# Key sums with v as the stationary side, two heads side by side, and token sums added on GpSimd

## The chip, the cores and the metric

The kernel runs on one core of one Trainium2 chip. The metric is the device time of one execution in microseconds, as the median of several runs; lower is better. The inputs are fp32 and come from a fixed seed.

## The reference

Random-feature attention over 8 batches of 8 heads with 576 tokens and head size 64, followed by a softplus MLP. The features are exp of a projection on 128 directions, less half the squared norm, less the row's maximum. Per head, the keys' features give a matrix `kv` (128 x 64) and a vector `z` (128), the sum of the features over the tokens.

```python
proj = np.einsum('bhsd,md->bhsm', x, omega)
h = proj - np.sum(x * x, axis=-1, keepdims=True) / 2.0
phi = np.exp(h - np.max(h, axis=-1, keepdims=True)) / np.sqrt(m)
kv = np.einsum('bhsm,bhsd->bhmd', k_p, v)
z = np.sum(k_p, axis=2)
num = np.einsum('bhsm,bhmd->bhsd', q_p, kv)
den = np.einsum('bhsm,bhm->bhs', q_p, z)[..., None] + 1e-06
x = (num / den).transpose(0, 2, 1, 3).reshape(B * S, H * D)   # 4608 x 512
g = softplus(x @ w_in)                                        # 512 -> 2048
out = g @ w_out                                               # 2048 -> 512
```

## The kernel before

**Work and tiles.** The MLP takes its 4608 tokens in blocks: two of 256, then eight of 512. For each block and each of 16 chunks of the hidden layer, TensorE computes layer 1 (`plan_step`, L1412 to L1414), ScalarE and VectorE compute the softplus, and TensorE adds the chunk to layer 2 (L1441 to L1443). Each operand is split in a high and a low part of a reduced fp32 format, so three products stand for one. The last two blocks are done as a pair with seven products in place of eight (`plan_pair`).

The attention is done in quads: four heads of one batch, 16 quads in all. A quad's tokens come in five units: units 0 to 3 hold 128 tokens of each of the four heads, unit 4 holds the last 64 tokens, with two heads on top of each other on the 128 partitions. The quads of the first batch have a path of their own (`plan_early_keys`, `plan_early_queries`); the change leaves it alone but for priorities. In the 14 later quads a unit is loaded, squared for its norms, projected (`plan_unit` for the second batch, `plan_split` with L588 from the third on), and its features are made by ScalarE (L495, L612).

**The sums over the keys** (`plan_sums`). For each later quad there are two bursts on TensorE, at L676: one over units 0 to 2, one over units 3 and 4. In a product the features of one head (128 tokens x 128 features) are the stationary side and v with a column of ones (65 columns) streams; unit 4 streams 130 columns for two heads, which are kept apart by zeros in v. The operands are full fp32, and the profile shows two instructions for each product. The result has features on the partitions and, for each head, 64 columns of `kv` and one column of `z`. ScalarE takes the first burst's result out of PSUM (`part`, L682). VectorE adds the second: `z` (L686) and `kv` (`whole`, L694). The four columns of `z` are turned by a 32 x 32 transpose (L690), go to DRAM in four transfers (L700), and come back spread over all partitions (L704). A query unit multiplies its features with that and sums (`den`, L784), takes the reciprocal (L790), divides (L794, on GpSimd or VectorE), turns blocks of 32 (L798), and goes through DRAM (L808, L821) to the products with `kv` (L954, L997, L1048): there 64 columns of `kv` are stationary, and the two heads of a pair write the upper and the lower 64 partitions of one bank.

**What sets the order.** Nothing is scheduled by hand. Each piece of work is put on a list with `do(engine, cost, due, emit, after=..., take=..., give=...)`; `in_order` runs through the list with a simple model of the engines (costs, lags, free buffers) and issues, on each engine, among the works that can start the one with the earliest `due`. The `due` numbers and the tables at the top (`KEYS`, `QUERIES`, `IN`, `OUT`) are the priorities. `take` and `give` name buffers; a buffer is free again when the work that gives it is done. The order that comes out is fixed at build time, and each engine executes it in order. GpSimd and VectorE share a port: each GpSimd work waits for the last VectorE work marked `port` that was issued ahead of it.

Of the kernel before, what the change touches and what calls it, by code (L numbers as in the profile page):

```python
# [50 lines left out]
KEYS = ((-130.35, -33.11, -44.26, -126.91, -51.00), (-184.12, -170.41, -56.38, -80.88, -261.61))  # L51
QUERIES = ((-121.36, -68.53, -68.01, 5.46, 8.94), (-154.85, -144.78, -170.95, 8.02, 66.23))
IN = (-77.35, -86.63, -115.20, 17.77, 69.89, -10.45, 6.40, 31.06, 149.98, 21.85, 124.48, 208.49, 408.59, 38.21, 62.49, 277.15)
OUT = (-17.17, 0.51, -6.07, 4.04, -17.23, 9.28, 112.67, 220.08, 30.78, 8.68, 46.33, 97.42, 71.82, 129.46, 148.54, 186.47)
# [47 lines left out]
def in_order(works, room, ahead, margin):  # L102
# [11 lines left out]
    first, out = 0, []  # L114
    port, queue, flying = [0.0, "POOL"], [0.0], [0.0] * MOST
# [28 lines left out]
    while len(out) < len(works):  # L144
# [26 lines left out]
        for box, key in w.give:  # L171
            free[box[key]] = w.done, e
            held[box[key]][-1][1::2] = w.done + lag(e, "PE"), len(out)
# [36 lines left out]
def favor_softplus_kernel(ctx, tc, q0, k0, qx, qy, kx, ky, vv, om, wi, wo, out):  # L210
# [57 lines left out]
    z_wide = [at.tile([P, 32], F32, name=f"z{i}") for i in range(2)]  # L268
    for t in z_wide:
        nc.vector.memset(t, 0.0)  # L270

    stack = const.tile([P, D], F32, name="stack")
# [42 lines left out]
    def plan_weights(nm, fc, due):  # L315
# [36 lines left out]
        def low_part(e):  # L352
# [5 lines left out]
            "SP", dma(0.65, 1.60, 1.7), due + 87.17, load, spare={} if last else {"w": 2},  # L358
# [5 lines left out]
        a = do(("ACT", "DVE"), (aw + 0.03, dw2), due + 3.12, low_bits, after=[l], port=True)  # L364
        b = do("ACT", aw + 0.03, due + 18.05, rebias, after=[l])
        c = do("DVE", dw, due + 9.50, joined, after=[a, b], port=True)
        d = do(
            ("ACT", "DVE"), (aw, dw2), due + 19.59, high_part, after=[c] + (in_w if last else []), take=[("w", box, "w")], port=True,
# [3 lines left out]
        return do(("DVE", "POOL"), (dw, pw), due - 0.32, low_part, after=[d], give=[(box, "raw")], port=True)  # L372
# [13 lines left out]
    def plan_unit(q, kind, us, due, early):  # L386
# [32 lines left out]
        def load_v(i):  # L419
            b["v", i] = wide(at.tile([P, 272], F32, name=f"v{nm}_{i}", tag=b["vs", i], bufs=1))  # L420
            nc.sync.dma_start(b["v", i], vv[q.b - 1, q.qd][:, 4 * us[i] : 4 * us[i] + 4])
# [8 lines left out]
        def norms():  # L430

            sm = b["sm"] = at.tile([P, 4, 8], F32, name=f"sm{nm}", tag=b["sms"], bufs=1)
# [230 lines left out]
    def plan_sums(q, keys, due, deps):  # L663
# [4 lines left out]
        def outer(k):  # L668
            b, i, u = keys[k]
            if not k:  # L670
                y["kv"] = wide(bank(f"kv{q.nm}_{q.sums}_{first}", y["bank"]))
# [1010 lines left out]
```

## Time and profile before

| | before |
|---|---|
| median of 3 runs | 996.43 us (996.05 to 996.76) |
| span of the profiled execution, first to last instruction | 995.2 us |
| median of the runs less that span | 1.2 us |
| TensorE busy | 989.6 us, 99% |
| weight loads of TensorE busy | 830.9 us, 83% |
| VectorE busy | 783.6 us, 79% |
| ScalarE busy | 722.7 us, 73% |
| GpSimd busy | 206.4 us, 21% |
| granted clock of TensorE, mean | 1.000 of full speed |

The busy times are sums over one execution that the profiler recorded. The profile gives no separate device time for that execution, so its span is set beside the median of the runs. Weight loads run beside products and have a row of their own. In the rows below PE is TensorE, PEld its weight loads, DVE VectorE, ACT ScalarE, POOL GpSimd and SP the engine that issues the transfers. In a timeline a row that ends in x16 is a run of 16 instructions of one line; matmuls overlap, so the start of the next row, and not the duration, says how long a run held the engine.

### The profile page before, as it was taken

The numbers are of one execution on the slowest core, as the hardware profiler recorded it, in microseconds if no ns is written. First come the engines' busy times: TensorE is split into PE (matmuls) and PEld (weight loads), VectorE is DVE, ScalarE is ACT, GpSimd is POOL, SyncE is SP. The second block draws the span as 40 slices with busy tenths as digits, with TensorE's granted clock in tenths as the row PEclk, the third lists the DMA queues.
The fourth block names the chain that finished last, engine by engine and source line by source line (L and its number), as shares of the span: only waits on it lengthen the run. The fifth ranks groups of instructions, "written<-read, shape, count | busy, mean of one in ns | idle before, by whom it ended". The sixth has DMA issues, their size and how long they took to land.

```text
span 995.2 us, 17488 instructions
## 1 busy us (share of the span) xinstructions
PE 989.6 (99%) x5495; PEld 830.9 (83%) x5495; DVE 783.6 (79%) x2306; ACT 722.7 (73%) x1794; POOL 206.4 (21%) x235
## 2 busy tenths in 40 slices
PE   9999999999999999999999999999999999999998
PEld 8988888888888888888878888888888878888886
DVE  6899986889898888888879886887787958676620
ACT  7999887879777777877777776776776656666520
POOL 3313232312221122101212121112011214223000
PEclk9999999999999999999999999999999999999999
DMA  9982355454464455543454444434542331000011
GB/s 321 352 282 90 111 162 152 138 160 141 136 183 139 125 138 160 159 128 113 138 144 133 123 129 119 155 106 113 138 141 75 80 92 43 0 1 1 1 43 42
DMA packets 117628, 124.49 MB, mean 125 GB/s; under 512 B 16288, under 2 KB 93728, under 8 KB 117536
## 3 DMA queue, kind: packets, MB, share of 16 engines
q1 hardware_dynamic: 117392, 123.26, 41.4%
q8 instruction: 43, 0.70, 0.3%
q14 instruction: 49, 0.40, 0.1%
q10 hardware_dynamic: 144, 0.13, 0.0%
HBM read 97.37 MB, written 25.98 MB: 124 GB/s over the span
## 4 chain that ended last, share of the span: by engine, by line
PE 98%; DVE 1%; ACT 0%; issue 0%
PE banks L1441 11%; PE banks L1412 11%; PE banks L1442 10%; PE banks L1443 10%; PE banks L1413 10%; PE banks L1414 10%; PE banks L1199 8%; PE banks L676 5%; PE banks L588 5%; PE banks L1256 3%; PE banks L1258 3%; PE banks L1257 3%; PE banks L445 2%; PE banks L997 2%; PE banks L735 1%; PE banks L954 1%
## 5 line engine op out<-in xcount | busy, mean ns | idle before, releaser
L1412 PE MATMUL banks<-xh,wi 128*128 128x512 f32 (+1 forms) x512 | 188.8, 369 | 0.4 <-DVE u L1427 0.4
L1413 PE MATMUL banks<-xl,wi 128*128 128x512 f32 (+1 forms) x512 | 186.1, 363 | 0.0
L1414 PE MATMUL banks<-xh,wi 128*128 128x512 f32 (+1 forms) x512 | 185.9, 363 | 0.0
L1441 PE MATMUL banks<-wo,gh 128*128 128x512 f32 x448 | 178.6, 399 | 0.0
L1442 PE MATMUL banks<-wo,gh 128*128 128x512 f32 x448 | 175.5, 392 | 0.0
L1443 PE MATMUL banks<-wo,gl 128*128 128x512 f32 x448 | 175.0, 391 | 0.0
L1418 ACT ACTIVATE u<-banks 128x512 f32<-128x512 f32 (+1 forms) x128 | 70.1, 548 | 73.4 <-PE banks L1414 60.5
L1412 PEld LDWEIGHTS banks<-xh,wi 128*128 128x128 f32 x512 | 96.4, 188 | 17.2 <-issue 1.2
L1414 PEld LDWEIGHTS banks<-xh,wi 128*128 128x128 f32 x512 | 96.4, 188 | 15.6
L1413 PEld LDWEIGHTS banks<-xl,wi 128*128 128x128 f32 x512 | 96.6, 189 | 13.9
L1441 PEld LDWEIGHTS banks<-wo,gh 128*128 128x128 f32 x448 | 84.2, 188 | 18.5 <-issue 4.3
L1443 PEld LDWEIGHTS banks<-wo,gl 128*128 128x128 f32 x448 | 84.1, 188 | 18.5
L1442 PEld LDWEIGHTS banks<-wo,gh 128*128 128x128 f32 x448 | 84.4, 188 | 13.3
L1427 DVE SCALAR_TENSOR_TENSOR u<-banks,u 128x512 f32<-128x512 f32 (+1 forms) x128 | 78.4, 613 | 15.8 <-ACT u L1424 15.4
L612 ACT ACTIVATE phq<-phq,smq 128x128 f32<-128x128 f32 x216 | 71.8, 395 | 14.7 <-DVE smq L608 14.7
L794 POOL TENSOR_TENSOR phq<-phq,dnq 128x512 f32<-128x512 f32 (+1 forms) x46 | 41.9, 911 | 189.2 <-DVE dnq L790 113.1
L612 ACT ACTIVATE phk<-phk,smk 128x128 f32<-128x128 f32 x216 | 71.9, 397 | 10.7 <-DVE smk L608 10.7
L784 DVE CUSTOM_DVE_ANT_0 restq<-phq,zb 128x128 f32<-128x128 f32 x280 | 72.7, 293 | 4.8 <-ACT phq L612 4.0
L1421 ACT ACTIVATE u<-u 128x512 f32<-128x512 f32 (+1 forms) x128 | 74.4, 581 | 1.8
L1424 ACT ACTIVATE u<-u 128x512 f32<-128x512 f32 (+1 forms) x128 | 74.6, 584 | 1.3
L1431 ACT CAST gh<-u 128x512 fp32r<-128x512 f32 (+1 forms) x97 | 55.8, 576 | 18.0 <-PE banks L1442 17.1
L1435 POOL TENSOR_TENSOR gl<-u,gh 128x512 fp32r<-128x512 f32 (+1 forms) x41 | 45.1, 1101 | 106.4 <-ACT gh L1431 31.5
(224 smaller groups left out, 2097.3 us busy)
## 6 DMA issues: line engine op xcount, KB each, us to landing
xk<-ky SPq DMA_DIRECT2D x48, 384.0 KB
xq<-qy SPq DMA_DIRECT2D x48, 384.0 KB
qdq<-restq SPq DMA_DIRECT2D x56, 256.0 KB
out<-o SPq DMA_DIRECT2D x36, 256.0 KB
vk<-vv SPq DMA_DIRECT2D x70, 130.0 KB
rawi<-wi SPq DMA_DIRECT2D x16, 512.0 KB
rawo<-wo SPq DMA_DIRECT2D x16, 512.0 KB
q<-qdq SPq DMA_DIRECT2D x64, 128.0 KB
```

The source lines that it names most:

```text
L612: nc.scalar.activation(b["ph"][:, c], b["ph"][:, c], AF.Exp, bias=b["sm"][:, 2, c : c + 1])
L784: i = nc.vector.tensor_tensor_reduce(jk[r, c], ph[r, c], q.zb[r, h], 1.0, 1e-6, ALU.mult, ALU.add, dn[r, 0, c : c + 1])
L1199: nc.tensor.matmul(b[key], x, y, start=fresh and not kk and not n, stop=kk == 1 and n == 2, skip_group_check=True)
L1412: nc.tensor.matmul(b["h"], wh, xh[:, cc, t], start=cc == 0, stop=False)
L1413: nc.tensor.matmul(b["h"], wh, xl[:, cc, t], start=False, stop=False)
L1414: nc.tensor.matmul(b["h"], wl, xh[:, cc, t], start=False, stop=cc == NCC - 1)
L1421: nc.scalar.activation(b["u"], b["u"], AF.Exp, scale=-1.0)
L1424: nc.scalar.activation(b["u"], b["u"], AF.Ln, bias=1.0)
L1427: nc.vector.scalar_tensor_tensor(b["u"], b["h"], 0.0, b["u"], ALU.max, ALU.add)
L1441: nc.tensor.matmul(acc[tt], gh, w2[fc][:, 0], start=fc == 0, stop=False)
L1442: nc.tensor.matmul(acc[tt], gh, w2[fc][:, 1], start=False, stop=False)
L1443: nc.tensor.matmul(acc[tt], gl, w2[fc][:, 0], start=False, stop=fc == NFC - 1)
```

## The change

For the 14 later quads the two sides of the key sums change places. v (64 columns of one head) is stationary and the features (128 columns) stream; the two heads of a pair write the lower and the upper 64 partitions of the same columns. Unit 4 has two products with 128 stationary columns, v of two heads side by side with zeros for the rows of the other head. The result has the columns of v on the partitions, so it is turned back by two TensorE transposes (`kv_turn`) after `part` and `whole`, and copied from PSUM to `kvs` by ScalarE or VectorE (`kv_turned`).

`z` is no longer a column of the products. GpSimd adds the features of the units into a tile for each quad (`plan_z`: unit 0 and 1, then 2, 3, and the two halves of unit 4). In `kv_turn` four products with a 128 x 32 block of ones add that up over the tokens, one head for each 32 partitions; ScalarE or VectorE copies the result (`z_row`), one transfer takes it to DRAM, and it is read back as before. The factor 1/128 of `z` moves into `den`. The buffers of the features are now given back by two works, the product and the addition, which `in_order` counts (`shared`). v is loaded with 64 columns in place of 65. Feature pieces of 320 tokens are loaded as 256 and 64. `z` has one buffer in place of two. All priorities have new values, and the rounding of the split units is put in a fixed order (`prev["rounded"]`).

```diff
-KEYS = ((-130.35, -33.11, -44.26, -126.91, -51.00), (-184.12, -170.41, -56.38, -80.88, -261.61))
+KEYS = ((-360.00, -109.33, -152.22, -165.69, -143.98), (-411.64, -277.96, -235.62, -203.68, -278.02))
...
         for box, key in w.give:
-            free[box[key]] = w.done, e
+            left, last = shared.get((id(box), key), (box.get(("uses", key), 1), (0.0, e)))
+            left, last = shared[id(box), key] = left - 1, max(last, (w.done, e))
+            if left:
+                continue
+            free[box[key]] = last
...
+    def plan_z(q, b, i, u, due, es):
+        b["uses", ("phs", i)] = 2
+        if not u:
+            q.z_first, q.z_slots = (b, i, es), {}
+            return
+        def add():
+            add_ = nc.gpsimd.tensor_tensor
+            x = b["ph", i]
+            if u == 1:
+                q.z = at.tile([P, 4, M], F32, name=f"z{q.nm}", tag="z", bufs=1)
+                b0, i0, _ = q.z_first
+                return add_(q.z, b0["ph", i0], x, ALU.add)
+            if u < 4:
+                return add_(q.z, q.z, x, ALU.add)
+            for j in (1, 0):
+                r, h = slice(j * D, (j + 1) * D), slice(2 * j, 2 * j + 2)
+                a_ = add_(q.z[r, h], q.z[r, h], x[r, :2], ALU.add)
+            return a_
...
+        q.z_last = do(
+            "POOL", pool(512) if u < 4 else 2 * pool(256), due - 200.04, add, after=after, give=give,
+            take=[("z", q.z_slots, "z")] if u == 1 else [],
+        )
...
         def outer(k):
...
-            for c in range(4 if u < 4 else 2):
-                end = k == len(keys) - 1 and c == (3 if u < 4 else 1)
-                cs = slice(c, c + 1) if u < 4 else slice(c, 4, 2)
-                nc.tensor.matmul(kv[:, cs], ph[:, c], v[:, cs], start=not k and not c, stop=end, skip_group_check=True)
+            end = k == len(keys) - 1
+            if u == 4:
+                for p in range(2):
+                    nc.tensor.matmul(kv[:, p], v[:, 2 * p : 2 * p + 2], ph[:, p], start=False, stop=end, skip_group_check=True)
+                return
+            for p in range(2):
+                for j in range(2):
+                    c = 2 * j + p
+                    nc.tensor.matmul(
+                        kv[j * D : (j + 1) * D, p], v[:, c], ph[:, c], start=not k and not p, stop=end, skip_group_check=True
+                    )
...
-        def z():
-            q.z = z_wide[int(q.slots["z"][-1])][:, :4]
-            nc.vector.scalar_tensor_tensor(q.z, y["kv"][:, :, D], rm, q.kvp[:, :, D], ALU.mult, ALU.add)
-        def z_turn():
-            nc.vector.transpose(q.zr, z_wide[int(q.slots["z"][-1])])
         def whole():
+            nc.vector.scalar_tensor_tensor(q.kvp, y["kv"], rm, q.kvp, ALU.mult, ALU.add)
+        def kv_turn():
+            y["turned"] = y["bank"][:, 2 * M :].rearrange("p (a m) -> p a m", m=P)
+            for p in range(2):
+                nc.tensor.transpose(y["turned"][:, p], q.kvp[:, p], ident)
+            for c in range(4):
+                nc.tensor.matmul(
+                    y["bank"][32 * c : 32 * (c + 1), :M], ones.broadcast_to([P, 32]), q.z[:, c], start=True, stop=True,
+                    skip_group_check=True,
+                )
+        def kv_turned(e):
+            (nc.scalar.copy if e == "ACT" else nc.vector.tensor_copy)(
+                q.kvs, y["turned"].rearrange("p a (j d) -> p (a j) d", d=D)
+            )
+        def z_row(e):
+            (nc.scalar.copy if e == "ACT" else nc.vector.tensor_copy)(q.z[:, 0], y["bank"][:, :M])
         def out_z():
-            for i in range(4):
-                r = slice(i * 32, (i + 1) * 32)
-                nc.sync.dma_start(q.zd[:, r], q.zr[i * 32 : i * 32 + 4])
+            nc.sync.dma_start(q.zd, q.z[::32, 0])
...
-        a = do("DVE", 0.1, due - 204.75, z, after=[m, q.part], take=[("z", q.slots, "z")])
-        q.kvl = do("DVE", 0.35, due - 85.10, whole, after=[m, a] + old, give=[(y, "bank")])
-        a = do("DVE", 0.11, due + 295.40, z_turn, after=[a])
-        r = do("SP", dma(2.0, 0.4, 1.4, 4), due - 43.15, out_z, after=[a], give=[(q.slots, "z")])
+        a = do("DVE", 0.35, due - 330.34, whole, after=[m, q.part])
+        y["uses", "at"] = 2
+        a = do("PE", 0.55, due - 96.36, kv_turn, after=[a, q.z_last], heat=512)
+        q.turned_kv = a
+        q.kvl = do(("ACT", "DVE"), (act(2 * P, PSUM), dve(2 * P)), due + 194.57, kv_turned, after=[a] + old, give=[(y, "at")])
+        a = do(("ACT", "DVE"), (act(M, PSUM), dve(M)), due - 364.83, z_row, after=[a], give=[(y, "at")])
+        r = do("SP", dma(2.0, 0.4, 1.4), due - 275.50, out_z, after=[a], give=[(q.z_slots, "z")])
...
-                        jk[r, c], ph[r, c], q.zb[r, h], 1.0, 1e-6, ALU.mult, ALU.add, dn[r, 0, c : c + 1]
+                        jk[r, c], ph[r, c], q.zb[r, h], 1.0 / M, 1e-6, ALU.mult, ALU.add, dn[r, 0, c : c + 1]
...
-            sizes = [w] if w <= 320 else [256, w - 256]
-            kinds = ["q" if w <= 256 else "q1"] if w <= 320 else ["q0", "q1"]
+            sizes = [w] if w <= 256 else [256, w - 256]
+            kinds = ["q"] if w <= 256 else ["q0", "q1"]
```

## Rows read from the trace of the kernel before

**Rows 1.** The page, part 1: busy us (share of the span) and instructions of each engine.

```profile
PE 989.6 (99%) x5495; PEld 830.9 (83%) x5495; DVE 783.6 (79%) x2306; ACT 722.7 (73%) x1794; POOL 206.4 (21%) x235
```

**Rows 2.** The page, part 4: the chain that ended last, by engine.

```profile
PE 98%; DVE 1%; ACT 0%; issue 0%
```

**Rows 3.** Waits of TensorE: total us, times, longest us (behind the first layer-1 product).

```profile
PE banks L1412 <- DVE u L1427: 0.4, 1, 0.4
```

**Rows 4.** Busy us by stretch: sum, PE, PEld, DVE, ACT, POOL, PEclk, DMA share, GB/s.

```profile
200.00:300.00 100.00, 100.00 (x539) 84.01 (x538) 90.24 (x287) 78.78 (x206) 22.00 (x24) 1.00 0.54 156
```

**Rows 5.** Timeline of TensorE, last product: start us, duration us.

```profile
990.98 0.39 PE L1258 MATMUL banks<-wo,wi 128*128 128x512 f32 x1
```

**Rows 6.** Timeline of TensorE around the two key-sum bursts of a quad.

```profile
196.30 0.39 PE L1414 MATMUL banks<-xh,wi 128*128 128x512 f32 x1
196.53 2.79 PE L676 MATMUL banks<-vk,phk 128*128 128x65 f32 x24
199.12 0.48 PE L1441 MATMUL banks<-wo,gh 128*128 128x512 f32 x1
199.44 0.39 PE L1442 MATMUL banks<-wo,gh 128*128 128x512 f32 x1
199.67 0.39 PE L1443 MATMUL banks<-wo,gl 128*128 128x512 f32 x1
...
212.99 1.50 PE L676 MATMUL banks<-vk,phk 128*128 128x65 f32 x12
214.25 0.48 PE L1441 MATMUL banks<-wo,gh 128*128 128x512 f32 x1
214.56 0.40 PE L1442 MATMUL banks<-wo,gh 128*128 128x512 f32 x1
```

**Rows 7.** Timeline of TensorE around three half-width bursts of query products.

```profile
668.90 0.39 PE L1443 MATMUL banks<-wo,gl 128*128 128x512 f32 x1
669.22 1.09 PE L954 MATMUL banks<-q,kvs 128*64 128x128 f32 x16
670.24 0.50 PE L1441 MATMUL banks<-wo,gh 128*128 128x512 f32 x1
670.58 0.40 PE L1442 MATMUL banks<-wo,gh 128*128 128x512 f32 x1
...
384.17 1.95 PE L954 MATMUL banks<-q,kvs 128*64 128x256 f32 x16
386.05 0.50 PE L1441 MATMUL banks<-wo,gh 128*128 128x512 f32 x1
...
719.78 0.39 PE L1443 MATMUL banks<-wo,gl 128*128 128x512 f32 x1
720.10 1.78 PE L997 MATMUL banks<-q,kvs 128*64 128x256 f32 x16
721.81 0.50 PE L1412 MATMUL banks<-xh,wi 128*128 128x512 f32 x1
722.15 0.40 PE L1413 MATMUL banks<-xl,wi 128*128 128x512 f32 x1
```

**Rows 8.** Timeline of TensorE, first batch: full-width fp32 products and transposes.

```profile
23.62 2.06 PE L735 MATMUL banks<-xk 128*128 128x128 f32 x16
25.52 0.60 PE L868 MATMUL banks<-ident,xq 128*128 128x128 f32 x4
25.95 1.04 PE L735 MATMUL banks<-xk 128*128 128x256 f32 x4
```

**Rows 9.** Groups by form, GpSimd: count, busy us, mean ns, idle before it.

```profile
L1435 POOL TENSOR_TENSOR gl<-u,gh 128x512 fp32r<-128x512 f32 x27 | 34.9, 1291 | 66.4 <-ACT gh L1431 17.9 <-DVE gh L1431 10.7 <-PE banks L588 9.7
```

**Rows 10.** Timeline of all engines: a second burst, and VectorE's sum behind it.

```profile
360.02 1.50 PE L676 MATMUL banks<-vk,phk 128*128 128x65 f32 x12
...
362.51 0.42 DVE L694 SCALAR_TENSOR_TENSOR kvs<-banks,kvp 128x256 f32<-128x256 f32 x1
```

**Rows 11.** Waits of all engines: GpSimd's division for VectorE's reciprocal.

```profile
POOL phq L794 <- DVE dnq L790: 113.1, 25, 13.1
```

More of the change, by code (lines that the diff above doesn't have):

```diff
@@ L933, in plan_early_x @@
         t = do(
-            "PE", 0.45 if tail else 0.46, due - 227.12, turn, after=[d for _, d in rows], heat=1024, behind=prev.get("turn_x"),
+            "PE", 0.45 if tail else 0.46, due - 244.69, turn, after=[d for _, d in rows], heat=1024, behind=prev.get("turn_x"),
             take=[("any", y, "b")], give=[(b, "x") for b, _ in rows],
@@ L1349, in plan_pair @@
-            q2 = do(*dp(2 * P), sdue - 139.44, lambda e, b=b: sums(e, 2, b), after=[q1, f1], port=True)
-            q3 = do(*dp(2 * P), sdue - 44.26, lambda e, b=b: sums(e, 3, b), after=[q2], give=[(b, ("tag", "f2"))], port=True)
-            q4 = do(*dp(2 * P), sdue - 32.45, lambda e, b=b: sums(e, 4, b), after=[q2], port=True)
+            sdue = due - 87.40
+            f1 = do(*dp(TB), sdue - 125.62, lambda e, b=b, j=j, nm=nm: whole(e, b, "f1", j, nm), after=gate + [done_w["i", j]], take=[("two", b, ("tag", "f1"))], port=True, behind=pe.get((5, j - 2)))
@@ new lines, in plan_pair @@
+            f2 = do(*dp(TB), sdue - 164.91, lambda e, b=b, j=j, nm=nm: whole(e, b, "f2", j + H, nm), after=gate + [done_w["i", j + H]], take=[("two", b, ("tag", "f2"))], port=True, behind=f1)
+            q1 = do(*dp(2 * P), sdue + 217.42, lambda e, b=b, nm=nm: sum1(e, b, nm), after=[f2], take=[("two", b, ("tag", "R"))], port=True)
+            q2 = do(*dp(2 * P), sdue - 274.51, lambda e, b=b: sums(e, 2, b), after=[q1, f1], port=True)
+            q3 = do(*dp(2 * P), sdue - 178.03, lambda e, b=b: sums(e, 3, b), after=[q2], give=[(b, ("tag", "f2"))], port=True)
@@ L1357, in plan_pair @@
+            l34 = do(*dp(TB), sdue - 353.47, lambda e, b=b, j=j: low34(e, j, b), after=[h34], give=[(b, ("tag", "f1"))], port=True)
             last = j == H - 1
             tg = [(late["tag"], ("th", p, l)) for p in range(2) for l in range(2)] if last else []
[L1359 to L1361 removed]
@@ new lines, in plan_pair @@
+            p7 = prod(7, "C", True, due - 337.85, [l34] + late["done"][3], kind=hp, give=tg)
+            s7 = do(*cp, due + 126.52, lambda e, b=b, nm=nm: copied(e, b, "C", "s7", nm), after=[p7], take=[("two", b, ("tag", "s7"))])
+            p5 = prod(5, "A", False, due - 128.66, [s2] + late["done"][1], give=[(b, ("tag", "L"))])
+            c22 = do("DVE", dve(TB), due - 123.42, lambda b=b: added(b["s7"], b["A"], b["s7"]), after=[p5, s7])
+            p4 = prod(4, "C", False, due - 160.26, [s7] + late["done"][4])
@@ L1481, in store @@
                 nc.sync.dma_start(out[t0 + tt * P : t0 + (tt + 1) * P, :], o["t"])
-            a = do("DVE", 0.34, due - 79.90, left, after=[ends[tt]], take=[("ph" if last else "t2", o, "s")])
-            r = do("ACT", 0.27, due - 143.96, right, after=[ends[tt]] if last and tt == n // P - 1 else [a], give=[(box, ("acc", i, tt))])
-            do("SP", dma(0.25, 0.8, 1.05), due - 76.25, store, after=[a, r], give=[(o, "s")], late=LATE["store"])
+            a = do("DVE", 0.34, due - 449.59, left, after=[ends[tt]], take=[("ph" if last else "t2", o, "s")])
+            r = do("ACT", 0.27, due - 458.35, right, after=[ends[tt]] if last and tt == n // P - 1 else [a], give=[(box, ("acc", i, tt))])
+            do("SP", dma(0.25, 0.8, 1.05), due - 370.79, store, after=[a, r], give=[(o, "s")], late=LATE["store"])
     assert NQ == 2
@@ L1522, in favor_softplus_kernel @@
     PAIR = 2
-    GAP = 1.58
-    PACE = 4.89
+    GAP = 5.05
+    PACE = 6.78
     t0, k, j = 0, 0, 0
```

278 lines of the change are left out of this document (140 added, 138 removed).

## The prediction

> **What bounds the kernel now.** I read the page first, for the busy shares: TensorE has 989.6 us of work in 995.2 us, 99%, against 79% on VectorE, 73% on ScalarE and 21% on GpSimd [rows 1]. A busy share can hide waits, so the next view was the chain that ended last: 98% of it is TensorE [rows 2]. Then the list of TensorE's own waits, to see whether anything ever keeps it: behind the first layer-1 product the longest is 0.4 us [rows 3]. Last, a table of stretches: in the hundred microseconds from 200 on TensorE is busy for all 100, while VectorE is at 90 and GpSimd at 22 [rows 4]. The reader is to see that the kernel is one queue of products without holes. A microsecond of TensorE work taken out is a microsecond of time, and one taken out elsewhere is worth nothing, unless its absence or presence opens a hole in that queue. All idle time of TensorE together is 995.2 - 989.6 = 5.6 us, and the last product starts at 990.98, 4.2 us before the end [rows 5], which leaves most of that to the closing copies and the store. So new priorities can win next to nothing by closing holes; they can only open some.
>
> The sum is therefore made from starts in TensorE's timeline: from when a burst may start to when the ordinary products run at their pace again. That pace is 0.23 us for a product of 512 columns (199.44 to 199.67 [rows 6]).
>
> **The key sums before.** Each of the 14 later quads has two bursts at L676. The one over three units (24 instructions, two for each product, since the operands are full fp32) starts at 196.53; the second product behind it starts at 199.44, so it takes 199.44 - 196.53 - 0.23 = 2.68 us. The one over the last two units takes 214.56 - 212.99 - 0.23 = 1.34 us [rows 6]. Together 4.02 us for a quad, 56.3 us for 14.
>
> **The key sums after.** Weights are now 64 columns of v, a product goes to the lower or upper half of the output partitions, and 128 columns of features stream. The nearest rows are the queries' products at L954, which have 64-column weights and alternate the same two halves. Eight products of 128 columns take 670.35 - 669.13 = 1.22 us (from the end of the pace before, 668.90 + 0.23, to 670.58 - 0.23); the same eight at 256 columns have 1.88 us from start to next start where those at 128 have 1.02 [rows 7]. So 128 columns cost (1.88 - 1.02) / 8 = 0.1075 us, which is half of what two full-width instructions of 128 columns cost below: two halves do run side by side. What does not shrink is a fee for each burst of 1.22 - 8 x 0.1075 = 0.36 us: a late start, a late return, and a drain. The fee isn't always that large: the burst at L997, eight products of 256 columns in another order, has 721.92 - 720.01 = 1.91 us, a fee of 0.19 [rows 7]. I take 0.36, because the new loop alternates the halves as L954 does, and keep 0.19 as the lower end.
>
> The Trainium skill says under "TensorEngine Tiling (Array Packing)", Tiling Modes, Key Properties, that changing the tiling mode drains the engine. The trace agrees with the direction: 0.19 to 0.36 us for each such burst, where the full-width burst returned after about 0.09. That rule speaks against this change, which adds mode changes to every quad; with no drain at all the sum below would come out some 15 us lower (an estimate: three fees of 0.36 for 14 quads).
>
> Burst of three units: 12 half-width products, 1.22 + 4 x 0.1075 = 1.65 us. Burst of the last two: four half-width products, 1.22 - 4 x 0.1075 = 0.79; then the tail unit, which keeps full-width weights (the zeros in v part the heads) and has two products of 128 columns, four instructions. Full-width instructions of 128 columns in full fp32 take (25.52 - 23.62) / 16 = 0.119 us [rows 8], so 0.48, and 0.08 for the return. That is 1.35 us, no better than the 1.34 before: in a short burst the fee eats the halving.
>
> **The turn, new.** Two transposes, at (25.95 - 25.52) / 4 = 0.108 us each [rows 8]: 0.22. Then four products of 128 columns with 32-column weights into the four quarters. No row shows a quarter-width product. If four run at once, they cost half of the half-width price, 4 x 0.054 = 0.21; two at once, 0.43; one after another, 0.86. I take four at once, since the two halves in [rows 7] do overlap fully, and keep the other two as ends. With one fee of 0.36 the turn is 0.79 us.
>
> **Sum on TensorE.** 1.65 + 1.35 + 0.79 = 3.79 us for a quad instead of 4.02: 0.23 less, 3.2 us less for 14. The split of the 320-column feature pieces into 256 and 64, at four places, leaves the columns as they are and can shift a fee by the 0.17 between the two kinds of burst; I put 0.2 us in for all of them. Net 3.0 us.
>
> **Off the path.** On VectorE the small token-sum and its 32 x 32 turn go; on ScalarE or VectorE two copies out of PSUM for each quad come. SP issues one store of the token sums for a quad instead of four. GpSimd gets four additions for a quad: three of 512 columns at 1.29 us (the price of L1435, a sum with two full inputs [rows 9]) and one in two halves, no less than 1.29 by the same row; 14 x 5.2 = 72 us, so some 280 us or 28%. All this costs nothing as long as the queue of TensorE stays full, and that cover is what I count on. If it goes, the price is in the second rival. The exclusive turns of GpSimd and VectorE may push a few sums from GpSimd to VectorE, which has about 10% left in the middle [rows 4].
>
> New on the path is a dependency: the turn sits in TensorE's in-order queue, behind VectorE's sum of the two parts and GpSimd's last addition. In one quad the VectorE work in that place (L694) ended at 362.93 where the burst had ended at 360.02 + 1.25 = 361.27, so 1.66 us later [rows 10]. If the order leaves the turn that long, it costs nothing; if it stands right behind the burst, up to 1.66. Everything queued behind it, the layers' products, would stand too. I take nothing, since nothing of this kind shows in [rows 3] today.
>
> **How it adds up.** The profiled execution has a span of 995.2; the median of the runs is 996.43, that is 1.2 us around the span. 995.2 - 3.0 + 1.2 = 993.4 us.
>
> **The rivals.**
> Smaller fees. If all three bursts pay 0.19 instead of 0.36, a quad saves 0.51 us more, 7.1 in all: 986.2 us. For it: the L997 bursts pay just that, and the mode change inside a burst may be cheaper than one against ordinary products. Against it: the new order of products is that of L954.
>
> The other side: GpSimd's sum is late at the turn. GpSimd works in order, and it waits a lot: 25 times for VectorE's reciprocal before a division, 113.1 us, mean 4.5, longest 13.1 [rows 11]. If a quad's last addition stands behind such a division, TensorE, which is now never kept, stands at the turn for about 4.5 us. One such wait gives 993.4 + 4.5 = 997.9, two give 1002.4. It decides from 5 us in all: below that it only eats the gain. For it: GpSimd had no work before on which TensorE's queue hung so directly in each quad. Against it: the products at L588 hang on GpSimd's remainders (L582) in the same way, and [rows 3] show no wait for them.
>
> The change doesn't do what it says: the quarter products overlap less. At two at once, a quad costs 4.00, and the time is 996.4, no change. At one after another it costs 4.44 against 4.02: 5.9 + 0.2 slower, 1002.5 us.
>
> **Chances and range.** My forecast (990.5 to 995.5): 0.46. Smaller fees, down to 986: 0.22. Quarter products without full overlap, 996 to 1002.5: 0.13. A late sum or turn: 0.19. What a measurement of this kernel can tell from no change is about 0.2%, 2 us. Faster by more than that: most of the forecast and all of the first rival, 0.62. Within it: the rest of the forecast, pairs at once, and one late sum, 0.20. Slower: 0.18. The range leaves out the far ends of the rivals: 985.5 to 1000.
>
> **What would show it.** A start-to-start time of 1.45 us or so for the 24 half-width instructions, and an ordinary product 0.1 us late behind them; a short burst no faster than before; a turn of ten instructions, eight of them within about 0.4 us; GpSimd near 280 us; no row over 0.5 us in TensorE's waits. The prediction is wrong if the wait list names the turn, if the fee of a burst isn't near 0.36, or if the stretch before the first layer-1 product has changed length by a microsecond or more.

## The result, and the profile after

The changed kernel takes 1007.58 us (median of four runs, 1004.82 to 1009.06) against 996.55 of the kernel before beside it: a ratio of 1.0105, 95% interval [1.009, 1.0121]. It is slower by some 11 us where 3 less were predicted. Its profiled execution has a span of 1007.3 us; it is the slowest of the four (1009.06).

The page of the changed kernel, busy times and the chain that ended last, then its waits of TensorE (in all, times, longest) and the stretch from 200 to 300:

```profile
PE 997.2 (99%) x5665; PEld 818.3 (81%) x5665; DVE 794.1 (79%) x2284; ACT 732.7 (73%) x1827; POOL 272.1 (27%) x292
PE 98%; DVE 1%; ACT 1%; issue 0%; ACTq 0%; DVEq 0%
```
```profile
PE banks L926 <- ACT xq L499: 3.1, 1, 3.1
PE banks L1629 <- DVE small L269: 1.1, 1, 1.1
PE banks L1470 <- ACT xh L986: 0.7, 1, 0.7
```
```profile
200.00:300.00 100.00, 100.00 (x559) 80.77 (x559) 86.05 (x265) 79.85 (x209) 32.13 (x33) 1.00 0.52 141
```

TensorE is still the one queue that sets the time, and behind 100 us it stands idle for 0.4 us in all (the rows of before are [rows 1 to 4]). No row names the turn. One wait is new and long: 3.1 us, for an exponent of an early query unit. The timeline of TensorE has it right behind the first layer-1 products (in brackets is the idle time before the row; the last row of the fence is the last product of the run), and the stretches show what the granted clock does behind it:

```profile
47.78 0.28 PE L1471 MATMUL banks<-xl,wi 128*128 128x256 f32 x1
47.90 0.28 PE L1472 MATMUL banks<-xh,wi 128*128 128x256 f32 x1
51.33 2.44 PE L926 MATMUL banks<-ident,xq 128*128 128x128 f32 x10 [3.14 <-ACT xq L499]
...
65.11 0.41 PE L1470 MATMUL banks<-xh,wi 128*128 128x256 f32 x1
65.33 0.41 PE L1471 MATMUL banks<-xl,wi 128*128 128x256 f32 x1
...
1002.85 0.39 PE L1316 MATMUL banks<-wo,wi 128*128 128x512 f32 x1
```
```profile
40.00:50.00 10.00, 8.18 (x83) 7.47 (x82) 9.37 (x28) 9.30 (x23) 3.53 (x3) 1.00 0.65 212
50.00:60.00 10.00, 8.68 (x43) 8.39 (x45) 7.42 (x21) 8.49 (x19) 2.91 (x3) 0.53 0.93 369
60.00:70.00 10.00, 9.18 (x62) 7.79 (x60) 7.21 (x20) 6.89 (x20) 3.85 (x3) 0.61 0.26 76
```

Products of 256 columns start 0.12 us apart at 47 us and 0.21 us apart at 65: the clock is at its lower level, 1.2 GHz, for 17 us in all, from 50.6, when TensorE has stood idle since 48.2, to 67.7. In the kernel before it stays at 2.4 GHz throughout this part, and the first layer-1 product starts at 53.33 instead of 45.77:

```profile
53.33 0.37 PE L1412 MATMUL banks<-xh,wi 128*128 128x256 f32 x1
```

The key sums themselves, on the same timeline, a long burst, a short one and the turn of one quad [rows 6 have those of before]:

```profile
254.67 0.39 PE L1501 MATMUL banks<-wo,gl 128*128 128x512 f32 x1
254.99 1.53 PE L721 MATMUL banks<-phk,vk 128*64 128x128 f32 x24
256.45 0.50 PE L1499 MATMUL banks<-wo,gh 128*128 128x512 f32 x1
256.79 0.39 PE L1500 MATMUL banks<-wo,gh 128*128 128x512 f32 x1
...
267.59 0.40 PE L1501 MATMUL banks<-wo,gl 128*128 128x512 f32 x1
267.92 0.66 PE L721 MATMUL banks<-phk,vk 128*64 128x128 f32 x8
268.50 0.71 PE L716 MATMUL banks<-phk,vk 128*128 128x128 f32 x4
268.97 0.47 PE L1470 MATMUL banks<-xh,wi 128*128 128x512 f32 x1
269.29 0.40 PE L1471 MATMUL banks<-xl,wi 128*128 128x512 f32 x1
...
270.21 0.40 PE L1472 MATMUL banks<-xh,wi 128*128 128x512 f32 x1
270.44 0.38 PE L737 MATMUL banks<-ident,kvp 128*128 128x128 f32 x2
270.75 0.43 PE L739 MATMUL banks<-z,small 128*32 128x128 f32 x8
271.11 0.50 PE L1470 MATMUL banks<-xh,wi 128*128 128x512 f32 x1
271.45 0.40 PE L1471 MATMUL banks<-xl,wi 128*128 128x512 f32 x1
```

Worked out as in the prediction: 256.79 - 254.90 - 0.23 = 1.66 us; 269.29 - 267.82 - 0.23 = 1.24; 271.45 - 270.44 - 0.23 = 0.78. Together 3.68 us for a quad, against 4.02 before; the other quads' bursts between 512-column products agree to 0.02 us. The eight instructions with 32 columns of weights take 0.36 us from their start to the next row's, where eight instructions of full width would take 0.95 (at 0.119 [rows 8]) and two at a time 0.48: four do run at once. (The Trainium skill says under "TensorEngine Tiling (Array Packing)", Tiling Modes, Key Properties, that tiles work independently of each other; the trace agrees for four tiles.)

So the change's own part gave what it was to give, and some 16 us were lost elsewhere. Counted from 100 us on, where the key sums differ: the last product starts at 1002.85 instead of 990.98 [rows 5], 11.9 us later. Of that:

- **Work left over from the head, 9.8 us.** At 100 us the changed kernel still has 42 more layer-1 products of 256 columns to run (0.119 us each) and 21 more layer-2 products (0.228); the rest of what is done by then, one quad's key sums among it, is the same in both.
- **Key sums, -4.4 us:** 13 quads at 0.34.
- **Slower ordinary products, 4.3 us.** Between 200 and 700 us two successive products of 512 columns start 230.74 ns apart on average (1569 pairs), where they were 228.72 before (1604 pairs). If that held for all 3171 such products behind 100 us it would be 6.4 us; a run with the same instructions in the same order and nearly the pace of before (e9_pad, below) needs 878.48 us from the product that starts at 120 us in the changed kernel to the last one, where the changed kernel needs 882.76, so I take 4.3.

The sum is 9.7; 2.2 us I can't assign. (The idle time behind 100 us is 0.4 of them; the query products, whose pieces the change splits, take 31.5 us from start to next start where they took 30.9; the 0.23 ns by which e9_pad's pace is still above that of before would be 0.7.) The experiments are about the first and the last of these three.

### The profile page after: what moved, and what is told of

It reads as the page before. It is cut to its first block, busy times and chain, and to the rows that moved or that the text cites. A ratio compares the mean times of both kernels' runs of the same rounds, so it can differ in the third digit from the quotient of the medians.

```text
span 1007.3 us, 17971 instructions
## 1 busy us (share of the span) xinstructions
PE 997.2 (99%) x5665; PEld 818.3 (81%) x5665; DVE 794.1 (79%) x2284; ACT 732.7 (73%) x1827; POOL 272.1 (27%) x292
## 4 chain that ended last, share of the span: by engine, by line
PE 98%; DVE 1%; ACT 1%; issue 0%; ACTq 0%; DVEq 0%
PE banks L1470 11%; PE banks L1499 11%; PE banks L1471 10%; PE banks L1472 10%; PE banks L1500 10%; PE banks L1501 10%; PE banks L1257 8%; PE banks L592 5%; PE banks L1314 3%; PE banks L1316 3%; PE banks L1315 3%; PE banks L721 3%; PE banks L449 2%; PE banks L1055 2%; PE banks L793 1%; PE banks L935 1%
## 5 line engine op out<-in xcount | busy, mean ns | idle before, releaser
L1470 PE MATMUL banks<-xh,wi 128*128 128x512 f32 (+1 forms) x512 | 191.6, 374 | 1.1 <-ACT xh L986 0.7
L1472 PE MATMUL banks<-xh,wi 128*128 128x512 f32 (+1 forms) x512 | 187.2, 366 | 0.0
L1489 ACT CAST gh<-u 128x512 fp32r<-128x512 f32 (+1 forms) x103 | 58.3, 567 | 33.5 <-PE banks L1500 29.7
L1493 DVE TENSOR_TENSOR gl<-u,gh 128x512 fp32r<-128x512 f32 (+1 forms) x101 | 66.9, 663 | 15.8 <-ACT gh L1489 12.2
L842 DVE CUSTOM_DVE_ANT_0 restq<-phq,zb 128x128 f32<-128x128 f32 x280 | 69.8, 291 | 6.0 <-ACT phq L616 4.9
L586 POOL TENSOR_TENSOR tq<-xq,tq 64x512 fp32r<-64x512 f32 (+1 forms) x31 | 34.0, 1097 | 101.3 <-ACT tq L582 20.8
```

The lines of the kernel that those rows point to most:

```text
L1470: nc.tensor.matmul(b["h"], wh, xh[:, cc, t], start=cc == 0, stop=False)
L1472: nc.tensor.matmul(b["h"], wl, xh[:, cc, t], start=False, stop=cc == NCC - 1)
```

## The experiments

### Slower products: the place of tiles in memory

Nothing in the change touches the layers, and their waits are the same. What did move is where tiles lie. The pool with features and queries got other sizes, so every tile of the pool behind it starts 64 bytes elsewhere; among them `u` of the softplus and `gh` and `gl`, the stationary operands of layer 2. Three runs change nothing but an unused tile of 64 bytes:

```diff
 # e1_shift, on the changed kernel: the second pool's tiles back by 64 bytes
+    ff.tile([P, 16], F32, name="shift", tag="shift", bufs=1)
 # e3_before_shift, on the kernel before: both pools' tiles moved
-    at.tile([P, 16], F32, name="gap")
 # e9_pad, on the changed kernel: both pools' tiles moved by 64 bytes
-    at.tile([P, 16], F32, name="gap")
+    at.tile([P, 32], F32, name="gap")
```

> The changed kernel with 64 bytes of unused memory ahead of the buffers of u, gh and gl, so that they start where they did before, modulo 128 bytes; the order of the work is the same. Theory A (where the loss is: a wait and a slow clock ahead of 70 us, and ordinary products that run about 2 ns slower each because the stationary operands gh and gl moved by 64 bytes): the spacing of two ordinary layer-2 products behind 200 us goes from a mean of 231.5 ns back to about 228.5, some 6 us less, about 999 to 1001 us. Theory B (the key sums and GpSimd's additions slow the ordinary products down): the spacing stays at 231 ns, and the time at 1005 to 1009 us.

> The kernel before without its unused 64-byte buffer (gap), so that u, gh and gl start 64 bytes earlier, as in the changed kernel; nothing else differs. Theory A: layer-2 products go from a mean of 228.7 ns to about 231.5, some 5 to 7 us more, 1001 to 1003 us. Theory B: no change, 996 us.

> The changed kernel with the unused tile of 128 bytes alone, order untouched. Beside the run that moved layer 2's tiles alone (1003.5) it moves the features, queries and copies too. If only the place of layer 2's stationary tiles matters: the same, 1003 to 1004.5. If the rest of the wider spacing (about 1 ns a product, 2.9 us) comes from the place of what the other engines read and write: 1000.5 to 1002.

The tile of 64 bytes taken out of the kernel before costs it 3.3 us (997.1 beside it): 1000.39 us, ratio 1.0035 [1.0023, 1.0046], with no new wait and the clock at its upper level. Its products then start 230.57 ns apart, as in the changed kernel. The other way round, e1_shift brings the changed kernel to 1003.54 us, 1.007 [1.0055, 1.0085], and 229.54 ns; e9_pad to 1002.86, 1.0065 [1.0048, 1.0082], and 228.95 ns, 0.2 above before. Of 2.0 ns lost, 1.2 came back with the second pool, that is with the stationary tiles of layer 2 and `u`, and 0.6 more when the first pool (features, queries and copies) moved as well. The first two runs moved less than I had expected (999 to 1001, and 1001 to 1003). From the same product (at 120 us) to the last, with the same instructions in between, the changed kernel takes 882.76 us, e1_shift 879.19 and e9_pad 878.48; e3_before_shift takes 874.66 where the kernel before takes 870.94.

The difference is small in the timeline: six layer-1 products behind the same four query projections take 1.39 us from start to start in the changed kernel (258.42 to 259.81) and 1.36 in e9_pad (255.61 to 256.97). No single row tells it: only a mean over hundreds of starts does, or the run. Layer 1 loses with layer 2, though its own operands have the same addresses in the changed kernel, e1_shift and e9_pad: its mean step there is 229.9, 229.3 and 229.0 ns (228.5 before), that of layer 2 is 231.7, 229.7 and 229.1 (229.0 before). So the place of a product's own operands can't be all of it; how the place acts stays open.

A rival for the same loss was GpSimd: it has 70 more additions (14 quads of five instructions), whose reads and writes could disturb the products. e8_thin cuts two of a quad's additions to one column for each head, which leaves the token sums short.

```diff
 # e8_thin, on the changed kernel
+            if 1 < u < 4:
+                return add_(q.z[:, :, :1], q.z[:, :, :1], x[:, :, :1], ALU.add)
```

> The changed kernel with two of GpSimd's four additions of each quad cut to one column of each head (they stay in their places in the order; the token sums are then left short): 28 additions fall from 1.3 us to about 0.1, so GpSimd works some 33 us less. Theory A (GpSimd's additions are hidden): no change, 1005 to 1009. Rival (the additions' reads and writes of memory slow the products or hold VectorE's turns): the spacing of the ordinary products goes back towards 228.7 ns and the time falls by half of what the wider spacing costs or more, 1001 to 1004.

1006.46 us, 1.0098 [1.0083, 1.0113], within the spread of the changed kernel's own runs, and 230.74 ns as before the cut, with 30 us of additions less: they are hidden, as the prediction had it.

### The head: the wait and the clock

The chain of waits of the changed kernel, in order of time (start, length, what), shows what stands between TensorE and its exponent, and VectorE's timeline why:

```profile
48.24 0.66 ACT xq L499 x2
48.90 0.51 ACT wi L354
...
51.00 0.28 ACT xq L499
51.33 2.44 PE banks L926 x10
```
```profile
46.68 0.68 DVE L348 SCALAR_TENSOR_TENSOR rawi<-rawi 128x512 uint32<-128x512 uint32 x1
...
47.35 1.28 DVE L348 SCALAR_TENSOR_TENSOR rawo<-rawo 128x512 uint32<-128x512 uint32 x2
48.55 1.28 DVE L348 SCALAR_TENSOR_TENSOR rawi<-rawi 128x512 uint32<-128x512 uint32 x2
49.76 0.15 DVE L488 SCALAR_TENSOR_TENSOR smq<-banks,smq 128x2 f32<-128x2 f32 x1
```

The new order puts five joinings of weights (L348) ahead of the last step of a maximum (L488, 0.15 us), and casts of weights (L354) ahead of the exponent. Is that the price of the order? The first test gives the changed kernel the priorities of before, and the kernel before the new ones (some 120 lines of numbers, no work touched). With them goes one number that is no priority, the cost of a key-sum burst on TensorE that the order is worked out with: 0.86 us a unit before, 0.50 after. The second test fills the hole.

```diff
 # e2_old_order; e5_new_order is the reverse, on the kernel before
-KEYS = ((-360.00, -109.33, -152.22, -165.69, -143.98), ...
+KEYS = ((-130.35, -33.11, -44.26, -126.91, -51.00), ...
...
 # e4_fill: 14 products on zeros ahead of the seventh early turn
+        if hasattr(w, "early_turn"):
+            turns += 1
+            if turns == 7:
+                fill(w.take[0][1]["tpb"], 14)
```

> The changed kernel with the priorities of the kernel before, wherever a work has one there (the turn takes that of the sum it follows, -85.10 for the turn's copy, -204.75 for the token row). Theory A: the wait of 3.1 us and the slow clock ahead of 70 us come from the new order, so both go; about 3 to 8 us less, 999 to 1004 us, with the products still at 230 to 231 ns. Theory C (the new work itself makes the wait, in whatever order): no row over 1 us in TensorE's waits goes away, and the time stays within 2 us of the changed kernel's.

> The kernel before with the priorities of the changed one: the old key sums in the new order. Theory A (an order fits only the work it was searched for): holes open everywhere as they did for the new work in the old order, 1020 to 1060. Rival (the new order is the worse one by itself, by what its head loses): about 1004 to 1008 with no new waits behind 100 us.

> The changed kernel with 14 idle products of 512 columns, 3.2 us of work, put on TensorE ahead of the transposes for which it waits 3.1 us at 48 us, so that it does not stand idle. Theory A: the wait shrinks to nothing, the granted clock stays at its upper level between 50 and 70 us, and the time is that of the changed kernel's run whose clock did not fall, 1004 to 1005 us. If the slow clock cost nothing, because other engines were late there anyway, the time stays at 1007 to 1009 us.

Over the whole run both exchanges are far worse: 1024.01 us, 1.0273 [1.0256, 1.029], for the new work in the old order, and 1092.45, 1.0959 [1.0939, 1.0979], for the old work in the new. My expectation of the first (999 to 1004) was wrong, and that of the second (1020 to 1060) too low. Behind 100 us e2_old_order stands idle for 11.3 us and runs 35 idle products that its order put into gaps; its waits of TensorE are spread over the run:

```profile
PE banks L1470 <- DVE u L1485: 3.8, 5, 1.4
PE banks L592 <- DVE phk L601: 1.7, 1, 1.7
```

So neither order carries the other's work through the run. How much of that is the wrong cost of a burst isn't shown. The head, though, answers the question. Its stretch from 40 to 100 us, e2_old_order first, then e5_new_order with its wait:

```profile
40.00:100.00 60.00, 58.78 (x479) 52.10 (x477) 58.37 (x162) 58.92 (x158) 17.63 (x15) 1.00 0.54 188
```
```profile
40.00:100.00 60.00, 53.74 (x404) 47.11 (x404) 54.15 (x149) 53.52 (x139) 20.83 (x19) 0.91 0.53 182
PE banks L868 <- ACT xq L495: 3.1, 1, 3.1
```

The new work in the old order has no such hole: TensorE is idle for 1.2 us of 60, the clock stays at its upper level, the first layer-1 product starts at 53.50, and at 100 us 168 layer-1 and 65 layer-2 products are done (162 and 66 in the kernel before). The old work in the new order has the changed kernel's head: the same wait of 3.1 us, 6.3 us idle, the low clock from 51.8 to 62.0, and 125 and 42 products done at 100 us (120 and 45 in the changed kernel). The cost of a burst isn't the reason here, since the first key-sum burst comes at 73.06 us in the changed kernel and at 70.33 in e5_new_order, behind the hole. So the loss at the head goes with the priorities and not with the work.

The idle products bring 3.3 us: 1004.28, 1.0078 [1.0061, 1.0096], from four runs of which one took 1007.52; the pair of kernels with the 128-byte tile, below, shows it more clearly. The hole is then just as long, 14 x 0.227 = 3.2 us of nothing useful, so these 3.3 us are about what the lower clock had cost; the mean clock from 40 to 100 us goes from 0.86 to 0.97. The spread of the changed kernel's own runs says the same: 1009.06 us at a mean clock of 0.991, 1004.82 at 0.999.

Both repairs in one kernel, e11_fill_pad (the idle products and the 128-byte tile):

> The changed kernel with both single repairs that gave something: 14 idle products in place of the wait (the hole stays, the clock is held up) and the 128-byte tile (products back at their spacing). If the two losses are separate they add up: 1004.3 less 4 = 1000 to 1001, and what is left against the kernel before is then the hole itself, the rest of the head and what the key sums gave. If they overlap: 1002 or more.

999.18 us, 1.0027 [1.0017, 1.0038], 3.7 less than the tile alone (e9_pad). The two losses are separate and add up. What is left against the kernel before is 2.4 us.

### The head: links moved one by one

The hole itself was next. The order is a list, so a few works can be moved in it and the rest left alone. First the exponent and the step ahead of it (e6_pull), then the same with the 128-byte tile (e7_pull_pad), then the whole chain behind the wait (e10_chain), then what e10 had shown to be late (e12_chain2). TensorE's own order changes in the last alone. The list is that of e12_chain2; where it has `put(327, 364, 336, 342)`, e10_chain has `put(319, 336, 342)`.

```diff
 # numbers are places in the list; put(a, b, c) moves b and c right behind a
+    put(261, 289)            # VectorE: last step of the maximum            e6, e7, e10, e12
+    put(274, 294, 296)       # ScalarE: its two exponents                   e6, e7, e10, e12
+    put(283, 299, 302, 304, 303, 306, 311, 310, 313, 324)  # turns, copies  e10, e12
+    put(300, 323, 330); put(312, 328, 331)                 # divisions      e10, e12
+    put(297, 335)            # GpSimd: squares of the next unit             e12
+    put(327, 364, 336, 342)  # VectorE: first activation, last division     e12
+    put(329, 368, 376); put(333, 370, 380)   # 12 layer-1 products earlier  e12
```

> The changed kernel with three small works moved in the order written out: VectorE's last step of the maximum of one early query unit (0.15 us) now stands ahead of five joinings of weights, and ScalarE's two exponents of that unit (0.68 us) ahead of the eight of the next units, in a place where ScalarE was idle for 0.7 us. TensorE's own order is the same. Theory A (the new order makes the loss at the head: TensorE waits 3.1 us for that exponent at 48 us, and the granted clock falls behind it): the wait goes down to 0.8 us or less, the clock stays at its upper level, and both prices come back, 3.3 us for the clock (as with the idle products) and some 2.5 for the wait: 1001 to 1002.5. Theory B (the low clock has another cause, or the wait only moves on to the next unit): 1005 to 1009, with a low stretch of 10 us or more left.

> The same move, and the unused tile at the head of the second pool made 128 bytes instead of 64, so that every tile behind it lies 64 bytes further: the stationary tiles of layer 2 are back where the kernel before had them, and the features and queries are moved too. If the two losses are separate, they add: 1001.5 less the 3.5 to 4 of the shifted tiles alone, 997 to 998.5. If the tiles of the features matter as well as those of layer 2, up to 2.9 us more: 994.5 to 997, ahead of the kernel before. If the head's loss is not what I take it for: 1001 to 1004.

> The changed kernel with the 128-byte tile at the head of the pool and the whole chain behind TensorE's wait at 48 us moved ahead of weights' works, not only its first link: for three early query units the exponents, the copies of the turned features (ScalarE) and the reciprocals and divisions (VectorE); TensorE's own order is again the same. Theory A (the loss at the head is the order on VectorE and ScalarE, which lets weights' works stand ahead of what TensorE needs next): no wait over 1 us between 46 and 56 us, no low clock there, and 2.5 to 5 us less than the run that moved the first link only (1001.0): 996 to 998.5. Theory C (VectorE and ScalarE have too much to do in this stretch whatever the order): TensorE's wait comes back behind 56 us as waits for the weights' works that were put off, 999.5 to 1001.5.

> The run before (128-byte tile, the first chain moved ahead of weights' works) gave 1002.0, since TensorE's wait came back at 54 us for GpSimd's squares of the next unit, which stand behind the low part of a weight that is needed 50 us later. Here those squares stand ahead of it, VectorE's last step of the first activation stands ahead of the maxima that wait for TensorE, and twelve layer-1 products, whose inputs are there, stand ahead of the projections on TensorE. Theory A (the order, which prepares weights long before their use and leaves products that could run behind works that can't): no wait over 2 us before 60 us, the low clock goes or shrinks to a few us, and 996.5 to 999. Theory C (VectorE and ScalarE have too much to do in this stretch whatever the order): the wait comes back once more, 1000 to 1003.

Measured: 1005.85, 1.0091 [1.0076, 1.0106]; 1001.01, 1.0044 [1.0029, 1.0059]; 1002.02, 1.0055 [1.0041, 1.0069]; 1002.54, 1.0058 [1.0044, 1.0072]. Against the same kernels without the moves (1007.58, and 1002.86 for the three with the tile) that is 1 to 2 us at most, no more than their runs spread by, and nothing from the longer chains. Had these works alone made the hole, I had expected 1001 to 1002.5, 997 to 998.5, 996 to 998.5 and 996.5 to 999. The first rows of each kernel's waits of TensorE show where the gain went; e7_pull_pad, e10_chain, e12_chain2 in turn:

```profile
PE banks L940 <- ACT xq L934: 2.8, 1, 2.8
```
```profile
PE banks L461 <- POOL xq L432: 3.0, 1, 3.0
PE banks L978 <- DVE xq L951: 1.7, 2, 1.1
```
```profile
PE banks L978 <- DVE xq L951: 1.9, 2, 1.3
PE banks L1470 <- DVE u L1485: 1.9, 2, 1.5
PE banks L926 <- ACT xq L499: 0.9, 1, 0.9
```

The wait walks. With the exponent early, the copies behind the turn are late (L934, 51 us); with these early too, GpSimd's squares (L432, 57 us); with these early too, divisions, activations and another exponent, in smaller pieces. The busy time of TensorE between 40 and 100 us stays the same: 55.40 us of 60 in the changed kernel, 55.72, 54.41 and 54.22 in these three, against 59.33 in the kernel before. Theory A, that the order of a few works makes this hole, fell: the priorities as a whole make it, as the exchange shows, and none of these moves undoes it.

### The head: is it too much work, or a chain

Either VectorE and ScalarE, which are about 90% busy in this stretch, have too much to do, or what TensorE needs comes through a chain of dependent steps that is long whatever these engines have to do. Three runs take work off the engines and leave order, waits and the number of instructions as they are (the weights, or the features too, then have other values).

```diff
 # e13_light on e9_pad, e14_before_light on the kernel before
-            low = box["low"]
+            low = box["low"][:, :16]
...
-                box["full"], box["high"], 3, box["low"], ALU.logical_shift_left, ALU.bitwise_or
+                box["full"], box["high"], 3, box["high"], ALU.logical_shift_left, ALU.bitwise_and
 # e15_light2: e13_light, and early maxima over 64 columns, sums of squares over 8
-            nc.vector.tensor_reduce(b["sm"][:, 1, j:n:2], b["pp"][j], AX.X, ALU.max)
+            nc.vector.tensor_reduce(b["sm"][:, 1, j:n:2], b["pp"][j][:, :, :64], AX.X, ALU.max)
```

> The changed kernel with the 128-byte tile (1002.9), and the step that scales the low words of the 32 weight tiles cut from 512 columns to 16 (the weights then lose their last bits and are joined from the high words alone, so they have other values; order, waits and the number of instructions stay). ScalarE and VectorE are relieved of 32 works of 0.4 to 0.65 us in the first 105 us, some 9 of 60 us between 40 and 100. Theory C (too much work on these two engines): TensorE's idle time between 40 and 100 us falls from 5.5 to under 3 us, no or little low clock, 998 to 1000.5. Theory D (a chain of dependencies or loads): it falls by less than 1.5 us, 1001.5 to 1003.

> The control: the same cut in the kernel before, whose TensorE has 0.7 us of idle time between 40 and 100 us. Both theories: 996 to 997.5. If it is faster by 2 us or more, the cut does something else than taking waits away, and the run beside it can't be read as meant.

> The run with the relieved ScalarE, and VectorE relieved too: in the early units the maxima are taken over 64 of 128 columns and the sums of squares over 8 of 64 (the features are then scaled by other factors), some 7 of the 13.5 us that these take between 40 and 100 us; they were 0.4 to 0.7 us each. The order stays. Theory E (VectorE's load, 94% of the stretch): TensorE's idle time between 40 and 100 us falls from 5.6 to under 3 us and more ordinary products are done by 100 us, 994 to 997. Theory D (a chain of dependencies through several engines, or loads, whatever the load): it stays over 4 us, 997 to 1000 as without it.

The table of the stretch from 40 to 100 us (sum, PE, PEld, DVE, ACT, POOL, clock) of the kernel before, the changed kernel, e13_light and e15_light2:

```profile
40.00:100.00 60.00, 59.33 (x463) 53.43 (x460) 57.41 (x161) 59.28 (x161) 14.91 (x14) 1.00 0.58 203
```
```profile
40.00:100.00 60.00, 55.40 (x417) 48.61 (x417) 52.65 (x143) 53.43 (x142) 20.93 (x19) 0.86 0.53 179
```
```profile
40.00:100.00 60.00, 54.45 (x466) 46.68 (x465) 56.20 (x154) 53.97 (x158) 21.47 (x20) 1.00 0.55 185
```
```profile
40.00:100.00 60.00, 55.01 (x463) 47.81 (x462) 51.21 (x152) 53.26 (x155) 21.71 (x20) 0.97 0.54 183
```

With VectorE at 51.2 us of 60 instead of 56.2, TensorE is idle for 5.0 us still; with ScalarE relieved alone, for 5.6. In the kernel before VectorE and ScalarE are busier than in any of them (57.4 and 59.3 us) and TensorE has 0.7 us of idle time. So it isn't the amount of work on these two engines: by the idle time theories C and E fell, and the chain (D), steps that wait for each other in the order that the new priorities make, is what remains. The times, 999.28, 1.0028 [1.0014, 1.0041], and 999.60, 1.0026 [1.0015, 1.0037], are 3.6 and 3.3 us under e9_pad (the first lies where theory C had it, 998 to 1000.5). That is mostly the clock, whose mean in this stretch is 1.00 and 0.97 instead of 0.94: the layer-1 product that starts at 100.07 us in e9_pad starts at 96.76 and 97.81, and TensorE is idle for as long as there (5.5 us) or 0.5 less. The control is 995.84, 0.9989 [0.9979, 0.9998], 1.3 us below its kernel: the cut gives little where there is no hole.

Which chain it is stays open. It can't be one link, since each link moved showed the next, and it goes through all four engines (exponent, turn, copy, product, division, sum, split, layer 1). An order of the new work without the hole is on record, that of e2_old_order, but it loses more behind 100 us than its head wins. Its head with the new priorities behind it was not run.

## Why the prediction was wrong

**The terms of the change itself were right.** Long burst 1.65 predicted and 1.66 measured, short burst 1.35 and 1.24, turn 0.79 and 0.78, so 4.8 us saved over 14 quads instead of 3.2. (The sum for the short burst had the return twice, in the fee of 0.36 and as 0.08 behind the tail.) Quarter-width products run four at once, as assumed. GpSimd's additions take 75.8 us (72 predicted), the engine 272 (280), and what e8_thin takes of them is hidden. The rival on the other side, a late sum at the turn, didn't come: no wait names the turn.

**The step that failed** is the one that gave the new order no price: "So new priorities can win next to nothing by closing holes; they can only open some", and, of the work off the path, "All this costs nothing as long as the queue of TensorE stays full, and that cover is what I count on." I had the direction and left it out of the sum and of the rivals, though the change searched all priorities anew. The cover is there from 100 us on and not ahead of it: at the head TensorE runs out of products for some 4 us more than before, and the lower clock that follows costs 3.3 us (e4_fill) to 4.2 (the spread of the changed kernel's runs) again. That the priorities do it is shown by the exchange: with those of before the new work has no such hole, and with the new ones the old work has it. The prediction had named the sign (a first layer-1 product moved by a microsecond or more; it moved by 7.6), but as something to look for afterwards, not as a case with a chance.

**A term that was missing** is the pace. "That pace is 0.23 us for a product of 512 columns" was taken as a property of the product. It depends on where tiles lie: a median of 227 ns between layer-2 products in a good place, 233 in a bad one, and the 2.0 ns between the means were worth 4.3 us here, nearly all that the key sums gave (4.8). A 64-byte tile alone shows it in the kernel before (e3_before_shift).

With both repaired as far as was found (e11_fill_pad), the key sums are still outweighed by what the head leaves over, and no version tried is faster than the kernel before.

## What to carry to other kernels

Where a kernel's order is written out by a search, a change of a few per cent of the work brings a whole new order, and its head, where no cover exists yet, has to be priced as a part of the change: compare what TensorE has still to do at a fixed early time, not only the waits. Exchange the priorities between the two kernels and read the head alone: it tells whether a loss there goes with the order or with the work, even if the runs as a whole get worse. Moving late links one by one didn't close the hole here. And after any change of tile sizes compare the mean distance of starts of instructions that were not touched: a shift of 64 bytes cost 3.3 to 4.3 us here, of the 4.8 that the change saves.

## What the hardware showed that I had not expected

- The distance between starts of fp32r products of 512 columns depends on the byte offset of tiles in a partition: with `gh`, `gl` and `u` at 192 modulo 256 the median step of layer 2 is 227 ns (228 in e1_shift), at 128 it is 232 to 233 (moving operands at 192 in both). Layer-1 products, whose operands stay at their addresses, slow down with them, by 0.6 ns on average between e1_shift and the changed kernel. Moving the first pool as well brought another 0.6 ns on average over both layers.
- Behind a single wait of 3.1 us the granted clock was at 1.2 GHz for far longer than the wait: 17 us in the changed kernel's profiled run, 10 in e5_new_order's, 6.8, in two parts, in e9_pad's. It isn't sure to fall: e13_light, with a wait of 2.7 us in the same place, kept 2.4 GHz there in its profiled run, and its ten runs lie between 997.38 us (mean clock 0.999) and 1003.15 (0.991).
- Eight instructions with 32-column weights, four products in four quarters of the output partitions, take 0.36 us together with the gap behind them.
